# First queries in one transposed load, V of group 0 behind them, K of group 1 after the first K

## The chip, the cores and the metric

One Trainium2 chip, one of its cores. The metric is the device time of one execution in microseconds (us), lower is better. Each time is a median over executions; every profile shows one execution.

## The reference

Grouped-query attention: 32 heads of queries share 8 heads of keys and values, so one "group" is 4 x 288 = 1152 rows of queries against one K and V of 512 rows.

```python
B, Hq, Hkv, Sq, Sk, D = 16, 32, 8, 288, 512, 128        # all bf16
k = jnp.repeat(k, Hq // Hkv, axis=1); v = jnp.repeat(v, Hq // Hkv, axis=1)
scores = jnp.einsum("bhqd,bhkd->bhqk", q, k) * D ** -0.5
p = softmax(scores, axis=-1)
return jnp.einsum("bhqk,bhkd->bhqd", p, v)
```

There are 128 groups, each cut into 3 steps of 1536 score columns: 384 steps.

## The kernel before

In each step PE makes the scores (`op_s`), ScalarE takes the exponential (`op_exp`), PE multiplies by V (`op_pv`, two steps later), and VectorE divides by the sums. Queries come by a transposed load, 9 tiles of 128 rows for a group. The K of groups 0 and 1 are loaded plainly and transposed on PE (`op_kt`).

```python
        def op_q0(i):                       # the first queries, in two loads
            c0, c1 = ((0, TB), (TB, NT))[i]            # TB = 4 tiles, NT = 9
            nc.sync.dma_start_transpose(qt_sb[:, 0, c0:c1], q_v[0:P, c0 * D:c1 * D]).then_inc(sem["s_qp%d" % i], 16)
...
        first = [lambda i=i: op_q0(i) for i in range(2)]          # SyncE's queue
        first += [lambda: op_q(1), lambda: op_k(0, 2), lambda: op_v(0, None, 1, UG), lambda: op_q(2), lambda: op_q(3)]
...
        @block.tensor
            op_warm(WARM, BANK, ps_o[:, 1])            # 5 dummy matmuls of 512 columns
            op_warm(1, P, ps_o[:, 1])
            op_kt(0, range(1), 0)                      # first K: transposes
            op_kt(0, range(1, NJ), 1)
            op_warm(1, P, ps_s[:, 1])
            for n in range(NS):
                op_s(n)                                # scores of step n
                ...
                if n == 1:
                    op_kt(1, range(NJ), 1)             # K of group 1
                if n >= LAG:                           # LAG = 2
                    op_pv(n - LAG)                     # outputs of step n - 2
...
        @block.scalar
            op_kd(eng, 0)                              # K of group 0, 128 KB
            op_v(0, eng, 0, 1)                         # V of group 0, 128 KB
            op_kd(eng, 1)                              # K of group 1, 128 KB
            eng.activation(dum[:], ..., ACTF.Exp)      # brings in the table
            for n in range(NS):
                op_exp(n)
```

The exponentials of steps 0 and 1 are cut into three of 512 columns, so that ScalarE can begin on a third of a step's scores.

## Time and profile before

| | kernel before |
|---|---|
| time, first three runs | 522.68, 522.98, 523.08 us |
| the profiled execution | **521.82 us**, span 520.1 us |
| ScalarE busy | 513.3 us |
| first exponential of the profiled execution | 5.27 us after the span's start |

The span lies inside the time: the time is about 1.7 us longer.

### The profile page before, as it was taken

How to read it: one execution, taken by the hardware profiler on the slowest of the kernel's cores; microseconds unless marked ns; L12 is line 12 of the kernel's file. 1: busy time of each engine (PE TensorE's matmuls, PEld its weight loads, DVE VectorE, ACT ScalarE, POOL GpSimd, SP SyncE). 2: the span in 40 equal slices, each digit the busy share in tenths (PEclk: the TensorE clock that was granted, in tenths of full speed). 3: DMA queues.
4: the chain of work that ended last, by engine and by line, in shares of the span. 5: the costliest groups of instructions: out<-in, count | busy, mean ns of one | idle time of the engine just before them, and what ended most of it. 6: DMA issues, size and time to landing. Idle time of an engine off the chain costs nothing.

```text
span 520.1 us, 15350 instructions
## 1 busy us (share of the span) xinstructions
PE 515.1 (99%) x6224; PEld 394.2 (76%) x6224; DVE 369.6 (71%) x1315; ACT 513.3 (99%) x393; POOL 79.4 (15%) x135
## 2 busy tenths in 40 slices
PE   8999999999999999999999999999999999999997
PEld 4777777777777777777777777777777777777776
DVE  2767767777777677776776776767767767677776
ACT  7999999999999999999999999999999999999997
POOL 2111111111111111111111111111111111111110
PEclk9999999999999999999999999999999999999999
DMA  9999999999999998999999989999999999997212
GB/s 179 237 181 265 274 183 247 235 215 211 245 210 260 210 253 183 234 227 242 235 240 190 222 229 225 238 184 224 220 231 229 225 205 199 219 226 177 90 69 93
DMA packets 253110, 110.06 MB, mean 212 GB/s; under 512 B 219760, under 2 KB 236784, under 8 KB 253040
## 3 DMA queue, kind: packets, MB, share of 16 engines
q1 hardware_dynamic: 252608, 108.69, 98.2%
q8 instruction: 49, 0.80, 0.7%
q10 hardware_dynamic: 432, 0.39, 0.3%
q14 instruction: 21, 0.17, 0.1%
HBM read 17.04 MB, written 37.75 MB: 105 GB/s over the span
## 4 chain that ended last, share of the span: by engine, by line
ACT 98%; DMA 1%; issue 1%; DVE 0%; PE 0%
ACT pt_sb L516 97%; DMA qt_sb<-in_q_dram 1%; ACT pt_sb L511 1%; DVE o_sb L585 0%; DVE o_sb L595 0%; PE ps_s L479 0%; PE ps_s L439 0%; DVE rl_sb L575 0%; PE ps_o L669 0%; DVE bad_sb L621 0%; DVE flag_i L733 0%; DVE bad_sb L618 0%
## 5 line engine op out<-in xcount | busy, mean ns | idle before, releaser
L516 ACT ACTIVATE pt_sb<-ps_s 128x1536 bf16<-128x1536 f32 (+2 forms) x384 | 508.8, 1443 | 0.0
L479 PE MATMUL ps_o<-v_sb,pt_sb 128*128 128x129 bf16 x4584 | 322.5, 220 | 0.4 <-ACT pt_sb L516 0.4
L479 PEld LDWEIGHTS ps_o<-v_sb,pt_sb 128*128 128x128 bf16 x4584 | 282.7, 98 | 50.2 <-DVE o_sb L585 14.1
L439 PE MATMUL ps_s<-qt_sb,kt_sb 128*128 128x512 bf16 (+2 forms) x1536 | 309.3, 324 | 1.0 <-DMA qt_sb<-in_q_dram 1.0
L585 DVE TENSOR_TENSOR o_sb<-ps_o,rl_sb 128x384 bf16<-128x384 f32 x382 | 211.9, 555 | 9.3 <-DVE rl_sb L575 0.5
L439 PEld LDWEIGHTS ps_s<-qt_sb,kt_sb 128*128 128x128 bf16 x1536 | 123.5, 98 | 62.3 <-DMA qt_sb<-in_q_dram 1.7
L575 DVE RECIPROCAL rl_sb<-ps_o 128x3 f32<-128x3 f32 x382 | 68.2, 178 | 126.4 <-PE ps_o L479 125.0
L568 POOL COPY v_sb<-vd_sb 128x512 bf16<-128x512 bf16 x128 | 78.4, 613 | 429.7 <-PE ps_o L479 416.2
L549 DVE SCALAR_TENSOR_TENSOR u_sb<-u_sb,m_sb 128x120 f32<-128x120 f32 x126 | 35.6, 283 | 2.2
L556 DVE SCALAR_TENSOR_TENSOR pt_sb<-u_sb,e_sb 128x120 bf16<-128x120 f32 x63 | 17.8, 283 | 2.2
L549 DVE SCALAR_TENSOR_TENSOR u_sb<-m_sb 128x120 f32<-128x120 f32 x63 | 17.5, 277 | 0.0
L527 DVE TENSOR_SCALAR y_sb<-ps_o 128x120 f32<-128x120 f32 x63 | 15.9, 253 | 0.0
L540 DVE TENSOR_SCALAR m_sb<-t_sb 128x120 int32<-128x120 int32 x63 | 14.1, 223 | 2.2
L450 PE MATMUL ps_o<-qt_sb,kt_sb 128*128 128x120 bf16 x63 | 13.6, 217 | 0.0
L540 DVE TENSOR_SCALAR e_sb<-t_sb 128x120 int32<-128x120 int32 x63 | 13.6, 216 | 0.0
L533 DVE TENSOR_SCALAR t_sb<-y_sb 128x120 int32<-128x120 f32 x63 | 13.4, 213 | 0.0
L450 PEld LDWEIGHTS ps_o<-qt_sb,kt_sb 128*128 128x128 bf16 x63 | 6.2, 98 | 7.4
L411 DVE COPY kt_sb<-ps_o 128x128 bf16<-128x128 bf16 (+2 forms) x3 | 1.0, 336 | 5.4 <-PE ps_o L404 5.3
L511 ACT ACTIVATE pt_sb<-ps_s 128x512 bf16<-128x512 f32 x6 | 3.3, 617 | 1.5 <-PE ps_s L439 1.5
L679 ACT ACT_TABLE_LOAD x1 | 1.3, 1283 | 2.2 <-issue 2.2
L613 DVE TENSOR_REDUCE st_sb<-rl_sb 128x1 f32<-128x72 f32 (+1 forms) x16 | 3.5, 217 | 0.0
L611 DVE TENSOR_REDUCE st_sb<-rl_sb 128x1 f32<-128x72 f32 (+1 forms) x16 | 3.5, 216 | 0.0
(32 smaller groups left out, 13.1 us busy)
## 6 DMA issues: line engine op xcount, KB each, us to landing
out_dram<-o_sb SPq DMA_DIRECT2D x127, 288.0 KB, 3.8
vd_sb<-in_v_dram SPq DMA_DIRECT2D x31, 512.0 KB, 5.3
qt_sb<-in_q_dram SPq DMA_TRANSPOSE x129, 5.0
kt_sb<-in_k_dram SPq DMA_TRANSPOSE x32, 5.0
vd_sb<-in_v_dram SPq DMA_DIRECT2D x1, 384.0 KB, 4.3
out_dram<-o_sb SPq DMA_DIRECT2D x3, 96.0 KB, 1.6
kd_sb<-in_k_dram ACTq DMA_DIRECT2D x2, 128.0 KB, 2.9
vd_sb<-in_v_dram ACTq DMA_DIRECT2D x1, 128.0 KB, 3.2
```

The costliest lines, as they stand in the source:

```text
L439: ins = emit(eng, w_x, lambda: eng.matmul(ps_s[:, n % 2, c:c + w], kt_sb[:, sl, j, gi, :], qg[:, t * P:t * P + w], start=True, stop=True))
L450: emit(eng, [("s_ev", n - LAG - 1)], lambda: eng.matmul(ps_o[:, (n - LAG) % 2, BANK - W:BANK], kt_sb[:, (g // UG) % NSLOT, j, g % UG, :], ...
L479: ins = emit(eng, w_x, lambda: eng.matmul(outs(r)[:, t - r % NC * TPC, :], pt(g, t, j), v_sb[:, sl, gi * NJ + j, 0:DV], start=(x == 0), st ...
L516: emit(eng, waits, lambda: eng.activation(d, s, ACTF.Exp, scale=scale)).then_inc(sem["s_e"], 1)
L527: emit(eng, [("s_yb", nth(n) - NB), ("s_pv", n - LAG + 1)], lambda: eng.tensor_scalar(out=y_sb[:, b], in0=ps_o[:, (n - LAG) % 2, BANK - W: ...
L533: emit(eng, [("s_ym", 2 * (nth(n) - NB)), ("s_y", nth(n))], lambda: eng.tensor_scalar(out=t_sb[:, b], in0=y_sb[:, b], scalar1=Y_MUL, scala ...
L540: emit(eng, [("s_yp", nth(n) - NB), ("s_yb", nth(n))], lambda: eng.tensor_scalar(out=dst[:, b], in0=t_sb[:, b], scalar1=mask, scalar2=bits ...
L549: lambda: eng.scalar_tensor_tensor(out=u_sb[:, b, x], in0=src, scalar=QUARTIC[x], in1=m, op0=ALU.add, op1=ALU.mult)
L556: lambda: eng.scalar_tensor_tensor(out=pt_sb[:, n % NPT, CH - W:CH], in0=u_sb[:, b, 2], scalar=QUARTIC[3], in1=e_sb[:, b].bitcast(FP32), o ...
L568: emit(eng, waits, lambda: eng.tensor_copy(v_sb[:, sl, gi * NJ:(gi + 1) * NJ, 0:D], vd_sb[:, sl, gi].rearrange("p (j d) -> p j d", d=D))). ...
L575: emit(eng, [("s_pv", r + 1)], lambda: eng.reciprocal(rl_sb[:, TPC * r:TPC * (r + 1)].unsqueeze(2), outs(r)[:, :, D:DV])).then_inc(sem["s_ ...
L585: emit(eng, waits, lambda: eng.tensor_tensor(out=o_sb[:, g % NO, t0:t0 + TPC, :], in0=outs(r)[:, :, 0:D], in1=rl_sb[:, TPC * r:TPC * (r + ...
```

## The change

The first scores wait for the first K and the first queries. The change lets these two transfers go alone. The queries come in one load of nine tiles, so that only one issue stands on SyncE's queue before V of group 0, which moves there. K of group 1 is issued when the first K has been copied out, and its transposes on PE move one step back.

```diff
         def op_q0(i):
-            c0, c1 = ((0, TB), (TB, NT))[i]
+            c0, c1 = 0, NT
...
-                return ("s_qp%d" % min(i, 1), 16)
+                return ("s_qp0", 16)
...
-        first = [lambda i=i: op_q0(i) for i in range(2)]
+        first = [lambda: op_q0(0), lambda: op_v(0, None, 0, 1)]
...
-                if n == 1:
+                if n == 2:
                     op_kt(1, range(NJ), 1)
...
             op_kd(eng, 0)
-            op_v(0, eng, 0, 1)
+            eng.activation(dum[:], nc.const_aps.tensor(0.0, [P, 1], FP32), ACTF.Exp)
+            for (s, n) in need(eng, [("s_k0", 2)]):
+                eng.wait_ge(s, n)
             op_kd(eng, 1)
-            eng.activation(dum[:], nc.const_aps.tensor(0.0, [P, 1], FP32), ACTF.Exp)
```

## The prediction

Its sum is -0.1 us (part 1) and about +0.05 us (part 5), hence 522.9 us.

> **What bounds the kernel now.** I read the busy table first, then the chain of work that ended last, then that chain for the first 20 us alone, then the merged timeline of the first 14 us, and last the landings of each early transfer. From the page:
>
> ```profile
> PE 515.1 (99%) x6224; PEld 394.2 (76%) x6224; DVE 369.6 (71%) x1315; ACT 513.3 (99%) x393; POOL 79.4 (15%) x135
> ...
> ACT 98%; DMA 1%; issue 1%; DVE 0%; PE 0%
> ...
> L516 ACT ACTIVATE pt_sb<-ps_s 128x1536 bf16<-128x1536 f32 (+2 forms) x384 | 508.8, 1443 | 0.0
> ```
>
> PE and ScalarE are both "99% busy", but the chain says whose time counts: the exponentials on ScalarE, with 0.0 us of idle before 384 of them. From the first exponential on, ScalarE never waits. So the span is (start of the first exponential) + (a fixed string of ScalarE work) + (a tail after it). The change touches neither string nor tail. It can move the time only by moving the first exponential, or by making a hole in the string near the start. The chain of the first 20 us shows what sets the first exponential:
>
> ```profile
> 0.82 3.97 DMA qt_sb<-in_q_dram
> 4.79 0.04 issue
> 4.84 0.41 PE ps_s L439
> 5.24 0.02 issue
> 5.27 1.08 ACT pt_sb L511 x2
> 6.35 0.49 ACT pt_sb L516
> 6.84 0.98 ACT pt_sb L511 x2
> 7.82 5.61 ACT pt_sb L516 x5
> ```
>
> Columns: start, length, what. The first half of the first queries (4 of 9 tiles) is issued at 0.82 and lands at 4.79; the first score matmul follows at once, the first exponential at 5.27. All that this change can win lies in these 5.27 us, 1% of the 520.1 us span. The other side of that wait, K, from the timeline:
>
> ```profile
> 0.82 0.38 ACTq L283 DMA_DIRECT2D kd_sb<-in_k_dram  x1
> 0.82 2.63 SPq L316 DMA_TRANSPOSE qt_sb<-in_q_dram  x2
> 1.23 0.45 ACTq L302 DMA_DIRECT2D vd_sb<-in_v_dram  x1
> 1.71 0.51 ACTq L283 DMA_DIRECT2D kd_sb<-in_k_dram  x1
> 2.25 1.28 ACT L679 ACT_TABLE_LOAD   x1 [2.25 <-issue]
> 3.34 0.34 PEld L404 LDWEIGHTS ps_o<-ident,kd_sb 128*128 128x128 bf16 x4 [0.67 <-DMA kd_sb<-in_k_dram]
> 3.67 0.68 DVE L411 COPY kt_sb<-ps_o 128x128 bf16<-128x128 bf16 x2 [2.72 <-PE ps_o L404]
> ```
>
> The first K lands near 3.3, is transposed on PE, and both copies out are done at 3.67 + 0.68 = 4.35. K is therefore ready 0.44 us before the queries (4.79). That 0.44 is about the most that earlier queries could win if K does not move.
>
> [...]the first transposed load shows 1.32 us on SyncE's queue and lands 3.97 us after its start. [...]by the packets of SyncE's queue, summed in 0.2 us windows, the first half's 512 packets of 256 bytes are through near 3.6 and the semaphore is seen at 4.79; the second half's last are through near 5.0 and it lands at 6.08. So 1.1 to 1.2 us lie behind the last packet[...].[...]
>
> **The change part by part.**
>
> 1. *One load of nine tiles in place of four and five.* It removes one issue from SyncE's queue (2.63 us for two, 1.3 for one). The first score matmul now waits for all nine tiles. What does a nine-tile load take? The rows of the queue show 77 single nine-tile loads after 60 us: the quickest, all with issues of 1.3 to 1.4 us, land after 3.4 to 4.0 us, mostly 3.6 or 3.7; the median over all is 5.0, under load. The early one of group 1 took 4.3 with an issue of 1.63. The four-tile half took 3.97. So size costs little and company much. By packets: the first starts at 2.3 (0.82 + 1.48); nine tiles are 1,152 packets, which group 1's load moved in about 1.4 us; plus about 0.2 for sharing with the first K until 2.5, plus 1.1 to 1.2: 2.3 + 1.6 + 1.15 = 5.05. By the quickest landings: 0.82 + 3.7 = 4.5. I take 4.7, between them and nearer the second[...]. Against 4.79: **-0.1 us**, uncertain by 0.3 either way.
>
> 2. *V of group 0 and K of group 1 leave the start of ScalarE's queue.* In the packet windows these two fill the engines from 2.9 to 4.2, at 70 to 95% of their time, while the packets of the queries fall from 95 to about 20 to 50 in 0.2 us. This is the company that the first load loses; it is counted in part 1. The first K lands no earlier, since the others came behind it: **0**.
>
> 3. *V of group 0 goes to SyncE.* Issue at about 2.1, for about 0.5 us; its packets come behind the queries', near 3.9 to 4.4; landing near 5.6; the GpSimd copy (613 ns) ends near 6.3. It is first needed by the first output matmul, which ran at 7.41. **0**. The loads behind it start about 0.8 us earlier than before (group 1's queries at about 2.7 in place of 3.51): slack, **0**.
>
> 4. *ScalarE waits for the copies of the first K before it issues K of group 1.* The wait ends at 4.35, the issue takes 0.4 to 0.5 us, so ScalarE is free at about 4.85. The first exponential needs the queries (4.7) plus 0.48, which is 5.18. The issue is hidden, by about 0.3 us. The table load (1.28) and the dummy move forward to 1.2 and are done before 3: **0**.
>
> 5. *K of group 1 comes later: 4.4 in place of 1.71.* A 128 KB load took 2.5 alone and 3.4 behind V; say 2.7 beside transposes: landing at 7.1 (earlier 5.1). The PE now transposes it after the scores of step 2, before the outputs of step 0. With the first exponential at T, step 2's scores end at T + 2.05: the third exponential ends at T + 1.6 (6.85 before), then four 128-column matmuls. Then transposes 0.39, outputs of step 0 0.84, scores of step 3 0.82 (three matmuls, the last one's full length): T + 4.1. The exponential of step 3 starts at T + 4.2 (9.47 before). Thus the scores come just in time, with 0.1 us of slack, if K has landed by T + 2.1. With T = 5.18 that is 7.28, against the estimated 7.1: **0**, but only just. A landing at 7.6 would open a hole of about 0.3 us.
>
> Sum: -0.1 (part 1) and about +0.05 as the mean of the hole in part 5 (about one chance in three of some 0.2). That is nothing that a time of 523 us shows.
>
> **Rivals.** (a) *The nine tiles land later than the four did*: the packet sum says 5.05, hence +0.25 us. For it speaks that half the data needs half the packets; against it, that the four-tile and nine-tile landings hardly differ in this trace. Result 523.2. (b) *K of group 1 takes the wait's place*: ScalarE stalls once before step 3. For it speaks the 0.1 us of slack; against it, that a lone 128 KB load landed in 2.5. Result up to 523.3. (c) *The unloaded start is as quick as the best later load*: landing at 4.3; then the first K (4.35) and ScalarE's own issue (4.85) bound it, the first exponential cannot come much before 4.9, and the win stops at 0.4 us. Result 522.6. (d) *DMA as the bound over the whole run*: the engines are about 98% busy in the slices, but ScalarE never waits for them; a shift of 0.8 us in the first loads changes nothing later. No effect.
>
> **Range and chances.** All branches lie within -0.4 to +0.6 us of the time before, 522.98, whose own three runs spread over 522.68 to 523.08. Point: 522.98 - 0.1 = 522.9. To hold run and chip differences too, 522.2 to 523.7. Two per cent would be 10.5 us, twice the whole start: faster 0.01, same 0.98, slower 0.01.
>
> **What would show it right or wrong.** In the changed kernel's chain of the first 20 us: the landing of the first queries (4.7; 4.79 before), the first exponential (5.2; 5.27), and whether anything stands between the exponentials of steps 2 and 3. In the timeline: ScalarE's second K issue at about 4.4, the transposes of that K at about 7.2, idle before them put down to its DMA. The string from the first exponential on should be as long as before. A start that moves more than 0.5 us, or any wait of ScalarE after 12 us, would make the prediction wrong in its mechanism; a string of exponentials with another mean than 1443 ns would make it wrong altogether.

## The result, and the profile after

The changed kernel took **521.73 us** (four runs, 521.47 to 522.01), the kernel before 523.03 us on the same chip (522.68 to 523.43). The ratio is 0.9975, with a 95% interval of 0.9958 to 0.9992. Ratios here are the mean time of one kernel's fast runs over that of the other's of the same rounds, so not quite the ratio of the medians. Against a threshold of 2% this is "same", as predicted; but 521.73 lies below the range of 522.2 to 523.7, and the change won about 1.3 us in this comparison where 0.1 was expected.

The page of the changed kernel still has ScalarE's exponentials as the chain, with no idle before them:

```profile
ACT 98%; DMA 1%; issue 1%; DVE 0%; PE 0%
...
L516 ACT ACTIVATE pt_sb<-ps_s 128x1536 bf16<-128x1536 f32 (+2 forms) x384 | 508.8, 1441 | 0.0
```

Its chain of the first 20 us (start, length, what):

```profile
0.82 3.54 DMA qt_sb<-in_q_dram
4.36 0.05 issue
4.41 0.62 PE ps_s L439
5.03 0.02 issue
5.05 1.09 ACT pt_sb L511 x2
```

The queries land at 4.36 in place of 4.79, the first exponential starts at 5.05 in place of 5.27. That is 0.22 us. The two profiled spans are 520.0 and 520.1, **0.1 us apart**. So the two traces do not show the 1.3 us at all. One detail shows where to look. The stretch from the landing to the first exponential has grown: one score matmul takes 0.62 here, 0.41 before. The merged timeline of PE's weight loads in the changed kernel tells the same:

```profile
4.81 0.15 PEld L439 LDWEIGHTS ps_s<-qt_sb,kt_sb 128*128 128x128 bf16 x1 [0.28 <-issue]
5.23 0.15 PEld L439 LDWEIGHTS ps_s<-qt_sb,kt_sb 128*128 128x128 bf16 x1 [0.28 <-issue]
5.66 0.15 PEld L439 LDWEIGHTS ps_s<-qt_sb,kt_sb 128*128 128x128 bf16 x1 [0.28 <-issue]
6.07 1.07 PEld L439 LDWEIGHTS ps_s<-qt_sb,kt_sb 128*128 128x128 bf16 x7 [0.26 <-issue]
```

Until about 6.1 the loads stand 0.43 us apart, one for each 512-column matmul, although nothing is waited for. Later they close up, and seven take 1.07. PE runs at half its rate until then. (Rate here means the spacing of 512-column matmuls: 0.43 us at half, 0.22 us at full, the latter from the first scores in the trace of before; what the trace itself records of the clock stands below, under "The clock that the traces record".) In the profiled execution of the kernel before, PE was already at full rate at its first scores (four weight loads in 0.55 us from 4.83).

### The profile page after: what moved, and what is told of

Read it like the earlier page. It is cut to its first block, busy times and chain, and to the rows that moved or that the text cites. A ratio compares the mean times of both kernels' runs of the same rounds, so it can differ in the third digit from the quotient of the medians.

```text
span 520.0 us, 15243 instructions
## 1 busy us (share of the span) xinstructions
PE 510.3 (98%) x6118; PEld 394.6 (76%) x6224; DVE 369.6 (71%) x1315; ACT 513.3 (99%) x393; POOL 79.8 (15%) x135
## 4 chain that ended last, share of the span: by engine, by line
ACT 98%; DMA 1%; issue 1%; DVE 0%; PE 0%
ACT pt_sb L516 97%; DMA qt_sb<-in_q_dram 1%; ACT pt_sb L511 1%; PE ps_s L439 0%; DVE o_sb L585 0%; DVE o_sb L595 0%; PE ps_s L479 0%; DVE rl_sb L575 0%; PE ps_o L669 0%; DVE bad_sb L621 0%; DVE flag_i L734 0%; DVE bad_sb L618 0%
## 5 line engine op out<-in xcount | busy, mean ns | idle before, releaser
L439 PE MATMUL ps_s<-qt_sb,kt_sb 128*128 128x512 bf16 (+2 forms) x1430 | 290.4, 320 | 5.0 <-DMA qt_sb<-in_q_dram 0.5
L417 PE MATMUL ps_o<-const-bfloat16-1.0 128*128 128x512 bf16 (+1 forms) x6 | 2.4, 570 | 0.9 <-PEq L752 0.9
```

Source lines behind the costliest of these rows:

```text
L439: ins = emit(eng, w_x, lambda: eng.matmul(ps_s[:, n % 2, c:c + w], kt_sb[:, sl, j, gi, :], qg[:, t * P:t * P + w], start=True, stop=True))
```

## The experiments

Kernels of one set ran on one chip with the kernel before beside them. I call an execution *early* when it took at most 522.2 us and *late* above that. For the kernel before, the 54 timed executions leave a gap there: none between 521.94 and 522.45. Every execution counts as "fast" by the cores' clock.

### First set: does the start vary, and which part does what?

**Both kernels again, unchanged** (no edit).

> The kernel before, unchanged, for its spread. The one profiled execution of before was 521.82 us (span 520.1), below all four timed ones (522.68 to 523.43). Theory P (start varies): most executions of before have a span near 521.3 because their first loads land later than in the profiled one; this profile, if it is of the 523 kind, shows the first exponential near 6.3 or a wait of ScalarE in the first 15 us, and the string after it as long as before. Rival C (chip): on one and the same chip before is 521.8 +- 0.3 in every execution and the change wins only the 0.2 us that the two traces show. Rival S (string): the string of exponentials or the tail is longer in the 523 executions.

> The changed kernel, unchanged, on the same chip. Theory P: 521.7, 1.0 to 1.4 us below before. Rival C: 0.2 us below before.

Before: 523.03 us (522.81 to 523.09, five executions), and 522.85 (521.87 to 523.42) for the eleven beside it, two of them early. After: 522.12 us (521.61 to 522.92, six executions), three early. The rival "chip" falls: one chip gives both kinds. So does the rival "string", for now there is a profile of a late execution. The chain of the first 20 us of before_again:

```profile
0.82 4.12 DMA qt_sb<-in_q_dram
4.95 0.04 issue
4.99 2.74 PE ps_s L439 x6
7.73 0.43 PE ps_o L404 x4
8.16 1.29 PE ps_s L439 x6
9.45 0.02 issue
9.48 5.31 ACT pt_sb L516 x4
```

The queries land at 4.95, only 0.16 later than in the first profile. From there the chain runs through PE: six score matmuls in 2.74 us, the transposes of K of group 1, six more score matmuls, at half rate (weight loads 0.43 us apart up to the one at 8.81). ScalarE gets through steps 0 and 1, then waits. Its list of waits names it:

```profile
ACT pt_sb L516 <- PE ps_s L439: 0.8, 1, 0.8
```

The span is 521.4: the first exponential is 0.37 later than in the first profile (5.64 for 5.27), and 0.80 us of hole comes before the third step. Theory P, "the start varies", held; its cause, late loads, was mostly wrong. after_again (span 520.8) has the same in small: first exponential at 5.14, holes of 0.35 and 0.19.

**One load alone**, everything else as before:

```diff
-            c0, c1 = ((0, TB), (TB, NT))[i]
+            c0, c1 = 0, NT
-                return ("s_qp%d" % min(i, 1), 16)
+                return ("s_qp0", 16)
-        first = [lambda i=i: op_q0(i) for i in range(2)]
+        first = [lambda: op_q0(0)]
```

> Before with the nine tiles in one load and nothing else changed: V of group 0 and K of group 1 stay at the head of ScalarE's queue. If the company of those two is what delays the first queries, the landing is no better than 4.8 to 5.3 and the time stays at 522.8 to 523.3. If the split into two loads costs the time, it falls to 521.7 to 522.0.

**The changed kernel with the queries in two loads**:

```diff
-        first = [lambda: op_q0(0), lambda: op_v(0, None, 0, 1)]
+        first = [lambda: op_q0(0), lambda: op_q0(1), lambda: op_v(0, None, 0, 1)]
```
(and `op_q0`, `have_q` as in the kernel before)

> The changed kernel with the first queries again in two loads, V of group 0 behind both. If the company on ScalarE's queue was the cause, the first half lands before 4.0, the first exponential is bound by K and ScalarE's own issue near 4.9, and the time is 521.5 to 521.8. If the split is the cause (a second load landing late, a hole in step 0 or 1), 522.5 to 523.

one_load: 523.41 us (523.14 to 523.63), all late, landing at 5.39. two_loads: 522.61 us (522.34 to 523.25); its first half is there by 3.8 and its first exponential starts at 4.52, the earliest of these four, yet ScalarE has holes of 0.41 and 0.74 us. The first is a wait for the queries of group 1, issued behind the second load and V. The second, before step 6, ends a chain through V of groups 1 to 3, which landed at 11.9 (in the first profile of before its copy could start at 10.85). The profiled execution also has a tail some 0.7 longer than the others, which I cannot explain; the other four have spans of 520.6 to 520.9.

The landings of the tiles that the first scores wait for, one profile each:

| | V of group 0 and K of group 1 beside it | alone with the first K |
|---|---|---|
| four tiles first | 4.79 and 4.95 | about 3.7 |
| nine tiles in one | 5.39 | 4.36 and 4.45 |

Company costs about 1.0 us, the five tiles more about 0.6. (Later profiles widen the table to 5.08 in its first cell and to 4.24 in its last.) The windows of the transfers from 2.8 to 3.0 us show it; q1 is SyncE's queue, q10 ScalarE's; packets, MB, share of 16 engines. The kernel before, then the changed one:

```profile
q1 hardware_dynamic: 90, 0.02, 56.4%
q10 hardware_dynamic: 12, 0.01, 25.8%
```

```profile
q1 hardware_dynamic: 201, 0.05, 130.0%
```

In this window the queries' packets move at less than half the pace in the kernel before, though only 12 packets of the other transfers fall in it (a quarter of the engines' time). It is one window of one execution: in before_again it holds 139 packets of the queries beside 5 of ScalarE's queue. Why company costs so much is not shown.

### Second set: is it PE's clock?

**Before with two dummy matmuls more**, to fill PE's idle time while it waits for the queries, and **after with one**:

```diff
             op_warm(1, P, ps_s[:, 1])
+            op_warm(2, BANK, ps_s[:, 1])       # before_fill2;  op_warm(1, ...) in after_fill1
```

> The kernel before with two dummy matmuls of 512 columns more, behind the transposes of the first K, so that PE has work while it waits for the first queries (its idle stretch was 4.1 to 5.0 us). Theory W (PE's clock): four of the six traces show score matmuls 0.43 us apart, not 0.22, until 6 to 10 us, and the slow ones have holes of 0.8 us before the third exponential; the clock comes up at a moment that varies, and later when PE idles before the first scores. Then [...]its spans lie between 520.1 and 520.7 and its median is near 522.1, 0.7 below before. Rival D (DMA): the holes come from late first loads and the filler wins nothing or costs up to 0.4: 522.9 to 523.3.

> The changed kernel with one such dummy matmul (its idle stretch is 3.9 to 4.45 us). Theory W: spans 519.9 to 520.5, median 521.8, so its slower executions (521.0 and more) vanish and it is only 0.2 to 0.4 below the kernel before with its two. Rival D: no gain, 522.1 to 522.5.

before_fill2: **522.03 us (521.94 to 522.14)**, six of six early, while the kernel before beside it spread from 521.82 to 523.65. after_fill1: **521.58 us (521.46 to 522.16)**, six of six early. Two useless matmuls take 1.0 us off the median of the kernel before, one takes 0.4 us off the mean of the changed kernel (pooled below), and most of the spread goes. Theory W, PE's clock, held against rival D. In before_fill2 the dummies end as the queries land (PE's timeline, then ScalarE's):

```profile
3.67 1.17 PE L417 MATMUL ps_s<-const-bfloat16-1.0 128*128 128x128 bf16 x3
4.85 1.99 PE L439 MATMUL ps_s<-qt_sb,kt_sb 128*128 128x512 bf16 x6
6.67 0.39 PE L404 MATMUL ps_o<-ident,kd_sb 128*128 128x128 bf16 x4
6.90 0.82 PE L439 MATMUL ps_s<-qt_sb,kt_sb 128*128 128x512 bf16 x6
```

```profile
6.94 1.10 ACT L511 ACTIVATE pt_sb<-ps_s 128x512 bf16<-128x512 f32 x2
7.90 8.61 ACT L516 ACTIVATE pt_sb<-ps_s 128x512 bf16<-128x512 f32 x7
```

The first six score matmuls are still partly slow, but full rate comes near 6, the second six take 0.82 in place of 1.49 (PE's timeline of before_again; 1.29 in its chain), and ScalarE has no hole.

**Before with only the move of the transposes**:

```diff
-                if n == 1:
+                if n == 2:
                     op_kt(1, range(NJ), 1)
```

> The kernel before with only one part of the change: the PE transposes K of group 1 behind the scores of step 2, not of step 1. Theory W: in executions with the slow clock the four transposes, 0.43 us, no longer stand before the scores of step 2, and the hole before the third exponential falls from 0.8 to about 0.4: median 522.5, 0.4 below before; in executions with the fast clock nothing changes. Rival: the transposes are hidden in either place: 522.9.

523.04 us (522.02 to 523.60), against 523.07: no gain, a miss for my figure of 0.4. In its profile full rate comes only at 10.4. The hole before step 2 is smaller, 0.37, but a second of 0.89 follows before step 3, as the transposes now delay the outputs and scores behind them. Moved, not removed.

**Before without its dummy matmuls at the start**:

```diff
-            op_warm(WARM, BANK, ps_o[:, 1])
-            op_warm(1, P, ps_o[:, 1])
...
-            op_warm(1, P, ps_s[:, 1])
```

> The kernel before without its eight dummy matmuls at the start. Theory W: PE works only from 3.4 to 3.9 and from 5.0 on, [...]ScalarE has holes before the exponentials of steps 2 and 3 or more (0.8 and up to 1.0 each): median 523.5 to 524.5, no execution below 522.7. Rival D: nothing changes, 522.9.

523.20 us (522.18 to 523.59), one of six early. Another miss in size: I had expected 523.5 to 524.5 and none below 522.7. The profile is of the expected kind (full rate at 10.4, holes of 0.79 and 0.45), but the median is only 0.13 above that of the kernel before beside it, far inside the noise (ratio 1.0002, interval 0.9986 to 1.0018). A worth of the dummies at the start is not shown.

### Third set: what keeps the clock low?

**The changed kernel and its filled version side by side**, unchanged.

> The changed kernel again, to be compared on one chip with the next three. Theory W2: [...]the changed kernel idles 0.45 to 0.65 us before its first scores, [...]so most executions are up early (spans 519.8 to 520.3) and some late (to 521.2): median 521.7 to 522.1.

> The changed kernel with one dummy matmul of 512 columns before its first scores, again. W2: all spans 519.8 to 520.5, median 521.6, at or below the changed kernel in every comparison and never above 522.3. Rival N (noise between chips): its median equals that of the changed kernel within 0.1 and its slow executions are as frequent.

What is left of theory W2: the shorter PE's idle time before the first scores, the more executions are early.

after_b: 521.86 us (521.47 to 522.76), four of six early. after_fill1_b: 521.67 us (521.50 to 521.84), five of five. In its profiled execution (span 520.1) K of group 1 stands in the chain: it landed at 7.57, later than the 7.1 estimated, and took about 0.2 us, which is the prediction's rival (b), small.

**The changed kernel without its dummies**, the same edit as before_nowarm.

> The changed kernel without its eight dummy matmuls. The kernel before lost only 0.1 to 0.2 without them (523.2). W2: there they were wasted, because the wait for the queries behind them kept the clock down in most executions; in the changed kernel they count[...]: median 522.5 to 522.9, a loss of 0.6 to 1.0, spans up to 521.4. Rival L (landing only): the change wins by its earlier start alone, and this loses 0.1 to 0.2 as before did: 521.9 to 522.2.

521.84 us (521.61 to 522.93), four of six early: no loss. My theory that the dummies at the start count only in the changed kernel is not borne out. At this number of executions no worth of them shows in either.

**Before with one dummy behind the transposes, not two**:

> The kernel before with one dummy matmul of 512 columns in place of two: it idles about 0.45 us before its first scores, as the changed kernel does. W2: at least half of the executions early (spans 520.2 to 520.5), some late (to 521.8), median 522.1 to 522.6. Rival L: the idle stretch does not matter at this size and most executions are late: 522.8 to 523.1.

522.06 us (521.73 to 523.15): four of five early, as expected. This points, on five executions, to the stretch just before the first scores.

### Fourth set and one run more: the company, and a faster version

**Only K of group 1 late**, and **only V of group 0 moved**:

```diff
             op_kd(eng, 0)
             op_v(0, eng, 0, 1)
-            op_kd(eng, 1)
             eng.activation(dum[:], ..., ACTF.Exp)
+            for (s, n) in need(eng, [("s_k0", 2)]):
+                eng.wait_ge(s, n)
+            op_kd(eng, 1)                       # k1_late; transposes at n == 2
```

```diff
+        first += [lambda: op_v(0, None, 0, 1)]  # v_late: behind both loads of queries
...
-            op_v(0, eng, 0, 1)
```

> The kernel before with K of group 1 alone taken from the start of ScalarE's queue (issued after the copies of the first K, transposed after the scores of step 2); V of group 0 stays. Landing of the first half of the queries: 4.8 before, 3.75 where both companions are gone. Theory E (each companion costs alike): 4.2. Theory V (V of group 0, first in line, is the one): 4.6 to 4.8. Theory K: 3.8 to 3.9.

> The kernel before with V of group 0 alone moved, behind the two loads of queries on SyncE's queue; K of group 1 stays at the start. Theory E: landing of the first half 4.2. Theory V: 3.8 to 3.9. Theory K: 4.6 to 4.8. A hole near step 5 from the late V of groups 1 to 3, as with the changed kernel in two loads.

k1_late: 522.86 us (522.09 to 523.07), scores from 4.85. v_late: 523.31 us (523.04 to 523.58), landing at 4.64. All three theories miss. By these profiles, one each, whichever companion stays costs nearly the whole 1.0 us; taking only one away wins 0 to 0.2. The change had to move both.

**A combination**: queries in two loads, K of group 1 late, V of group 0 on ScalarE's queue behind the table load, V of groups 1 to 3 before K of groups 2 and 3. Relative to the changed kernel, with the two-load `op_q0` and `have_q` again:

```diff
-        first = [lambda: op_q0(0), lambda: op_v(0, None, 0, 1)]
-        first += [lambda: op_q(1), lambda: op_k(0, 2), lambda: op_v(0, None, 1, UG), ...]
+        first = [lambda i=i: op_q0(i) for i in range(2)]
+        first += [lambda: op_q(1), lambda: op_v(0, None, 1, UG), lambda: op_k(0, 2), ...]
...
             eng.activation(dum[:], ..., ACTF.Exp)
+            op_v(0, eng, 0, 1)
```

> The queries in two loads, K of group 1 late as in the change, V of group 0 on ScalarE's queue but behind the table load (issue near 2.7), V of groups 1 to 3 before K of groups 2 and 3 on SyncE's queue. Theory W3 (the start is set by the landing of the four tiles, the rest by PE's idle stretch before the first scores, which this leaves no room for): first half lands near 3.8, first exponential at 4.5, no hole by V: every span 519.2 to 519.8, median 521.1, below the changed kernel with its dummy matmul by 0.4. If V behind the table load still disturbs the first half: landing 4.1 to 4.4, 521.3 to 521.6.

> The changed kernel with one dummy matmul more, on the same chip as the three above: 521.6, every execution below 522.3.

combo: 522.91 us (522.14 to 523.40). It missed its own condition. ScalarE's queue did not hold the issue back behind the table load (1.28 us from 1.23):

```profile
1.29 0.39 ACTq L302 DMA_DIRECT2D vd_sb<-in_v_dram  x1
```

So V of group 0 kept the first load company, which landed at 4.77. after_fill1_c, beside it: 521.55 us (521.49 to 521.75), four of four early.

**The combination with a wait**: ScalarE waits for the landing of the first K before it issues V of group 0.

```diff
             eng.activation(dum[:], ..., ACTF.Exp)
+            for (s, n) in need(eng, [("s_kd0", 16)]):
+                eng.wait_ge(s, n)
             op_v(0, eng, 0, 1)
```

> The run combo missed its condition: ScalarE's queue issued V of group 0 at 1.29, not behind the table load, and the first half landed at 4.77, as with two companions. Here ScalarE waits for the landing of the first K (3.2) before it issues V of group 0, so that nothing accompanies the first K and the first half of the queries. Theory W3: first half lands at 3.75, PE has no idle stretch before the first scores, first exponential at 4.5; V of group 0 lands near 6.2 and its copy is done by 6.9, in time for the outputs at 7.0; every span 519.2 to 519.8, median 521.1, no execution above 521.7. If the start does not set the time, or PE's clock is late all the same: 521.6 or more, with a hole on ScalarE.

522.77 us (522.00 to 523.53), two of six early (a third, at 522.24, just missed the limit): a miss. The first half landed early and the first exponential started at 4.51, as expected. But V, issued at 3.03, now kept the second half company:

```profile
2.20 4.31 DMA qt_sb<-in_q_dram
6.51 0.05 issue
6.56 1.95 PE ps_s L439 x8
```

That load took 4.31, PE stood idle for 1.60 us before the scores on it, and ScalarE had holes of 0.41, 0.47 and 1.06. PE was at full rate for its first scores and lost it again: its granted clock fell to half at 6.97 and was back at full only at 10.38. In these lines of `prof combo2 --windows` PE's busy time is the first number behind the comma, the clock the third from the end:

```profile
4.00:5.00 1.00, 0.96 (x4) 0.21 (x3) 0.08 (x1) 0.49 (x1) 0.00 (x0) 1.00 0.98 246
5.00:6.50 1.50, 0.00 (x0) 0.00 (x0) 0.00 (x0) 1.50 (x4) 0.61 (x1) 1.00 0.95 158
7.00:8.00 1.00, 1.00 (x5) 0.43 (x4) 0.00 (x0) 1.00 (x2) 0.00 (x0) 0.50 1.20 207
```

The version that beats both kernels is therefore the changed kernel with one dummy matmul.

### What the sets say together

The ten profiled executions of the first two sets and of the two originals, in us (the idle time is that of PE just before its first scores; the holes are ScalarE's, after its first exponential):

| profile | PE idle | first exponential | full PE clock recorded from | holes | span |
|---|---|---|---|---|---|
| before | 0.81 | 5.27 | 3.86 | 0 | 520.1 |
| before_again | 0.83 | 5.64 | 9.36 | 0.80 | 521.4 |
| after | 0.46 | 5.05 | 6.04 | 0 | 520.0 |
| after_again | 0.64 | 5.14 | 8.36 | 0.54 | 520.8 |
| one_load | 1.31 | 6.08 | 9.84 | 0.80 | 521.9 |
| two_loads | 0 | 4.52 | 5.50 | 1.15 (loads) | 521.6 |
| before_fill2 | 0 | 5.50 | 5.86 | 0 | 520.3 |
| after_fill1 | 0 | 5.04 | 6.37 | 0 | 519.9 |
| before_kt2 | 0.92 | 5.50 | 10.40 | 1.26 | 521.9 |
| before_nowarm | 0.97 | 5.50 | 10.38 | 1.24 | 521.9 |

Span less first exponential less holes is 514.8 to 515.2 in every row but two_loads, the one with the longer tail. So the string and the tail are as fixed as the prediction said; what varies is the first exponential and the holes.

**The clock that the traces record.** Every packed trace but that of k1_late holds stretches of the clock granted to PE (`clock` in trace.npz; the PEclk column is made from them). Before the first one nothing is recorded and the column prints 1.00, so it hides the slow start. The first, at full clock, begins where the matmuls close up (in before ahead of the scores): this is the fourth column of the table.

Set beside PE's idle time just before its first scores, over all profiles: the filled kernels had next to none (under 0.1 us), after_b 0.45 and after 0.46, and they were at full rate by 5.9 to 6.5. after_nowarm had 0.57, after_again 0.64, before_fill1 0.65, v_late 0.79, before_again 0.83, combo 0.89, before_kt2 0.92, before_nowarm 0.97 and one_load 1.31: half rate until 8.3 or later. two_loads and combo2, with no such idle time, were at full rate from 5.50 and at their first scores (3.77). Two do not fit, before with 0.81 and k1_late with 0.91, both at full rate at their first scores; in before the full clock is recorded from 3.86, ahead of the wait. So the idle time goes with a late clock, but does not settle it alone. What sets the moment at which the clock rises is not shown.

Pooled over all sets, on several chips:

| | executions | early | mean of early | mean of late | mean of all |
|---|---|---|---|---|---|
| before | 54 | 10 (19%) | 521.86 | 522.98 | 522.77 |
| after | 16 | 11 (69%) | 521.71 | 522.68 | 522.01 |
| after with one dummy | 15 | 15 | 521.63 | none | 521.63 |

The means of all differ by 0.76 us. Were the kernel before early in 69% of its executions, its mean would be 0.69 x 521.86 + 0.31 x 522.98 = 522.21. So 0.56 of the 0.76 comes from fewer late executions and 0.20 from the earlier start within each kind. The 1.3 us of the first comparison was larger because all four of its changed executions were early and all four of the others late.

## Why the prediction was wrong

**What failed is the first step**, the reading of the bound: "From the first exponential on, ScalarE never waits. So the span is (start of the first exponential) + (a fixed string of ScalarE work) + (a tail after it)." That is true of the profiled execution and of about one in five. In the late profiles of the kernel before and its close variants ScalarE waits for 0.6 to 1.3 us, because PE, at half rate, has the scores ready too late (by PE's timelines, 2.74 us for six score matmuls, 0.63 for the transposes and 1.49 for the next six in before_again, against 1.99, 0.39 and 0.82 in before_fill2, where ScalarE never waits for the later steps). The warning stood in the times: the profile belonged to an execution of 521.82, and the three runs began at 522.68. The prediction quoted 522.68 to 523.08 as spread and took 522.98 as its base for a trace that was not of that kind. Its answer, base less 0.1, could not come out right.

**Part 1, the landing**, was mis-sized: -0.1 predicted, with a landing at 4.7; measured 4.36 and 4.45, that is -0.3 to -0.4. Two terms were too large. I let the nine tiles take 1.6 us of packets; alone, they ran at 201 to 229 packets per 0.2 us from 2.8 to 3.6; the first half load of the kernel before had 90 to 109 from 2.4 to 3.2. And I added 1.15 us behind the last packet; from near 3.65 to 4.36 it was 0.7, so the time behind the last packet was not the same in the two kernels.

**Part 2, the company**, was seen in the right place but counted only where its packets were in the way, from 2.9 on. one_load and two_loads put it at 1.0 us, k1_late and v_late show that either companion alone costs nearly as much.

**Parts 3 and 4** held. The copy of V of group 0 started at 5.59 (predicted landing 5.6) and was waited for by nobody on ScalarE. ScalarE's issue at 4.27 took 0.33 and hid behind the first scores.

**Part 5** held in kind. K of group 1 landed near 7.3 in the first profile and at 7.57 in another (7.1 predicted), where it cost about 0.2 us. The move of its transposes was rightly worth nothing (before_kt2).

**The first exponential** was rightly expected to move by little, 5.27 to 5.2; it moved to 5.05, less than the landing, because the first matmul ran at half rate (0.62 us in the chain, 0.41 before). This gain alone, 0.2 us, would have left the prediction inside its range. None of the four rivals named PE's clock.

**What is shown and what is open.** Shown: ten of the eleven profiled late executions have PE at half rate until 8.3 to 10.4 us (in combo2 for a second time; the eleventh is two_loads, with its holes by loads); filling PE's idle time just before the first scores removes the late executions in both kernels; the changed kernel has a shorter such stretch (0.45 to 0.64 against 0.8 to 0.9) and fewer late executions. That the shorter stretch is why it has fewer is a reading of the filled kernels (21 of 21 early), of one_load (1.31 us of idle, none early) and of the idle times listed above; no run shows a limit for it. Open: what makes the clock rise at 3.86 us in one execution of the kernel before and at 9.36 in another (before, before_again), although PE began its fifth dummy matmul at 2.52 in both; and what brings it down again, seen once, at 6.97 in combo2 behind 1.60 us of idle. Open too: why a second transfer on the other queue slows the first load so much (about 1.0 us later here).

## What to carry to other kernels

Compare the profiled execution's own time with the timed runs before reading it: if it lies outside them, it is the profile of another case. Where PE feeds the engine that bounds the kernel, check the spacing of the first matmuls and the recorded clock, and fill PE's wait for the first data with dummy matmuls right up to the first real one; here one of 512 columns was worth 0.4 us in the mean and removed the spread. Let nothing be issued beside the transfer that everything waits for, on any queue (here company cost it about 1.0 us), and check that moving it does not put it beside the next one (in combo2 that one then took 4.31 us).
